# Softmax sums of the first block's heads taken from the four score chunks on TensorE, and later casts and w_out copies on ScalarE

## The chip, the cores and the metric

The kernel runs on one core of one Trainium2 chip. The metric is the device time of one execution in microseconds; a measured time is the median of several runs. Each core has TensorE (PE in the profile: matmuls and, as PEld, the loading of their weights), VectorE (DVE), ScalarE (ACT), GpSimd (POOL), and SyncE (SP), whose queue issues most transfers. Every engine works through its own instructions in the order in which they are written for it.

## The reference

Three layers follow one another: attention with capped scores, a feed-forward layer with a squared ReLU, and a mixture of experts with soft slots.

```python
def _attn_ref(q, k, v, cap):                 # q, k, v: (4, 12, 448, 64)
    scores = scale * np.matmul(q, k.transpose(0, 1, 3, 2))
    scores = cap * np.tanh(scores / cap)
    scores = scores - np.max(scores, axis=-1, keepdims=True)
    attn = np.exp(scores)
    attn = attn / (np.sum(attn, axis=-1, keepdims=True) + 1e-09)
    return np.matmul(attn, v).astype(np.float32)

def _moe_ref(x, w_in, w_out, s, b):          # x: (1792, 768), w_in: (768, 2048), w_out: (2048, 768)
    h = x @ w_in
    r = np.maximum(h, 0.0)
    g = s * (r * r) + b
    return (g @ w_out).astype(np.float32)

def _moe2_ref(x, phi, w1, w2):               # 8 experts, 4 slots each
    logits = x @ phi
    ...
    slot_input = d.T @ x                     # d: softmax of the logits over the tokens
    ...
        h = np.maximum(slot_input[e] @ w1[e], 0.0)
        slot_out[e] = h @ w2[e]
    ...
    return (c @ slot_out).astype(np.float32) # c: softmax of the logits over the slots
```

w_in and w_out come as 64-bit floats, and the kernel turns them into 32-bit ones itself.

## The kernel before

**Pairs of heads.** Attention goes by pairs of heads: 24 pairs, numbered 0 to 23, six for each of the four batch entries. One pair's scores are made in four chunks of 112 keys (`scores`, L111, tile `sc`), each chunk for both heads at once: six matmuls, because the operands q and k are each split into a high part rounded to the matmul format and a low rest (`split`, L72 the cast and L73 the subtraction; tiles `qh`, `ql`, `kh`, `kl`). ScalarE applies tanh to each chunk (L114), and after every second chunk exp to the two together (`expo`, L147); the result is the tile `e`, half 0 for the chunks 0 and 1, half 1 for 2 and 3.

**Softmax sums.** VectorE adds the four chunks into the tile `es` (`add`, L153 for half 0, L156 twice for half 1). `weighted` then makes, per pair, two matmuls of a block of ones with `es` (L165, tile `Sm`), whose 113th row holds the small constant of the reference, and eight matmuls of v with the chunks (L168, tile `U`, one accumulator). One head writes the upper and one the lower 64 partitions of both accumulators. A 32-bit matmul shows as two instructions in the profile. VectorE takes the reciprocal of `Sm` (L172), multiplies (L174), and splits the result into the tile `x` of the feed-forward layer (L72, L73).

**Stages.** In the opening stretch only attention runs: the six pairs of batch entry 0 and the first half of the scores of pair 6, with some of the weight conversion between (`convert`: a piece of w_in or w_out is loaded into `raw`, scaled by ScalarE at L228, and put together by VectorE at L233, L255 and L259; two `raw` buffers). Then come four blocks, one per batch entry: each has 16 chunks of the hidden layer (`hidden`, L380, tile `hp`; the weights are split at L364 by ScalarE and L365 by VectorE), mixed with the next batch entry's attention and with what follows the hidden layer. w_out's pieces are also turned on TensorE (`wturn`, L329, tile `tw`), copied back by VectorE (L331) and stored. In block 3 and behind it the expert weights are loaded and used.

**What sets the order.** A scheduler of the language orders each engine's instructions ahead of time, from the program's order and its own estimates. The chip then follows these lists. The tiles `sc` have two PSUM buffers in the opening stretch and one after it; `U`, `Sm` and the general bank `T` have one each.

Of the kernel before, what the change touches and what calls it, by code (L numbers as in the profile page):

```python
# [18 lines left out]
B, H, S, D = 4, 12, 448, 64  # L19
NP = H // 2  # L20
CP = 112
# [14 lines left out]
CAP_FAST = 40.0  # L36
GP = 3
STEPS = 8
LEAD = 4
U = 256  # L40
CU = 768
# [11 lines left out]
class Body:  # L53
# [14 lines left out]
    def bank(self, name):  # L68
        return self.pst[0].tile([P, 512], F32, tag="T", bufs=self.pst[1], name=name)

    def split(self, hi, lo, src):
        self.nc.vector.tensor_copy(hi, src)  # L72
        self.nc.vector.tensor_sub(lo, src, hi.bitcast(F32))  # L73

    def turns(self, tag, i, kept, more, last, shape, dt):
# [18 lines left out]
    def prep_pair(self, p):  # L94
        if p >= B * NP:
            return
        q2, k2, v = self.qk[p]
        t = [self.ap.tile([P, S], F32R, tag=n, bufs=2, name=n) for n in ("qh", "ql", "kh", "kl")]
        self.split(t[0], t[1], q2)
        self.split(t[2], t[3], k2)  # L100
        self.qk[p] = (*t, v)

    def scores(self, p, c):
# [54 lines left out]
    def weighted(self, p):  # L158

        nc, c = self.nc, self.c  # L160
        U = self.psa.tile([P, 512], F32, tag="U", bufs=1, name="U")
        Sm = self.psa.tile([P, 512], F32, tag="S", bufs=1, name="Sm")
        v = self.qk[p][-1]
        for i in range(2):
            nc.tensor.matmul(Sm[64 * i:64 * i + 64, :S], c["ones"][:CP + 1, :64], self.es[:CP + 1, i, :], start=True, stop=True)  # L165
        for k in range(NCH):
            for i in range(2):
                nc.tensor.matmul(U[64 * i:64 * i + 64, :S], v[:, i, k * D:(k + 1) * D], self.chunk(2 * p + i, k),  # L168
                                 start=(k == 0), stop=(k == NCH - 1))
        del self.qk[p], self.e[p]  # L170
        rec = self.ap.tile([P, S], F32, tag="rec", bufs=1, name="rec")
        nc.vector.reciprocal(rec, Sm[:, :S])  # L172
        u = self.ap.tile([P, S], F32, tag="u", bufs=1, name="u")
        nc.vector.tensor_mul(u, U[:, :S], rec)  # L174
        xt = self.xtile(p // NP)
        self.split(xt[:, 0, p % NP, :], xt[:, 1, p % NP, :], u)

    def xtile(self, bi):
        if bi not in self.x:
# [4 lines left out]
    def attention(self):  # L184

        for p in range(2):
            self.load_pair(p)
        self.prep_pair(0)
        self.es = self.ap.tile([P, 2, S], F32, name="es")
        self.nc.vector.memset(self.es, EPS)  # L190
        if not self.general:
            self.nc.vector.tensor_scalar(self.es, self.es, self.c["eps"], None, op0=ALU.mult)
        last = B * NP
        for p in range(last + 1):
            for k in range(STEPS):
                if p < last and k % 2 == 0:
                    if k == 0:
                        self.load_pair(p + 1)
                    self.scores(p, k // 2)
                    self.expo(p, k // 2)  # L200
                elif k == 3 and p:
                    self.weighted(p - 1)
                elif k in (5, 7) and p < last:
                    if k == 7 or not self.general:
                        for h in range(2) if self.general else (k // 7,):
                            self.add(p, h)
                    if k == 5:
                        self.prep_pair(p + 1)
                yield
# [68 lines left out]
    def conv_units(self):  # L278


        nc, io, c = self.nc, self.io, self.c
# [16 lines left out]
        def proj(fh, half):  # L298
            if half == 0:
                return  # L300
            o = cur.pop(("o", fh)).rearrange("p (a b) -> p a b", b=U)
            self.later = [lambda: down(fh, o)]
            if self.f64:
                self.later += [lambda th=th: wturn(fh, th, o) for th in range(3)]
            self.later.insert(2, lambda: fold(fh))
# [19 lines left out]
        def wturn(fh, th, o):  # L325
            tw = self.bank("tw")
            for j in range(2):
                for k in range(2):
                    nc.tensor.transpose(tw[:, (2 * j + k) * P:(2 * j + k + 1) * P], o[:, 2 * th + k, j * P:(j + 1) * P], c["idn"])  # L329
            n = o[:, 2 * th:2 * th + 2, :].rearrange("p a b -> p (a b)")  # L330
            nc.vector.tensor_copy(n, tw)  # L331
            nc.sync.dma_start(self.osc[th][:, 2 * U * fh:2 * U * (fh + 1)], n)
            self.wide = th < 2

# [184 lines left out]
    def run(self):  # L519
        nc, tc, c = self.nc, self.tc, self.c  # L520
        with ExitStack() as top:
            pool = lambda st, name, side, **k: st.enter_context(tc.tile_pool(name=name, bufs=1, side=side, **k))
            self.gp = pool(top, "gp", "left")
            with ExitStack() as mid:
# [8 lines left out]
                with ExitStack() as att:  # L533
# [5 lines left out]
                    with tc.tile_pool(name="ps2", bufs=1, space=PSUM, side="right") as self.ps2:  # L539
                        for k in range(NP * STEPS + 4):  # L540
                            next(atn)
# [26 lines left out]
    def block(self, bi, atn):  # L568
# [3 lines left out]
        last = bi == B - 1  # L572
        done, total = 0, 0 if last else NP * STEPS
        for grp in range(4):
# [6 lines left out]
            for k in range(12):  # L581
                next(h)
                next(post, None)
                if bi < 2:
                    next(self.conv, None)
                while done < min(total, (12 * grp + k + 1) * total / (48 - LEAD)):
                    next(atn)
# [232 lines left out]
```

## Time and profile before

| | |
|---|---|
| time, median of 3 runs | 693.3 us (691.75 to 693.62) |
| the profiled execution: its time, its span | 692.1 us, 690.2 us |
| TensorE busy | 629.7 us, 91% of the span |
| VectorE busy | 415.9 us, 60% |
| ScalarE busy | 383.5 us, 56% |
| granted TensorE clock, mean | 0.97 |

The span runs from the first to the last instruction of the trace; 1.9 us of the execution lie around it. A busy share is a mean over stages with different limits, and a TensorE that counts as busy may still be waiting inside a pipelined matmul, so the stages have to be read one by one. A granted clock of 1.00 is the level of 2.4 GHz, 0.50 that of 1.2 GHz.

### The profile page before, as it was taken

How to read it: one execution, taken by the hardware profiler on the slowest of the kernel's cores; microseconds unless marked ns; L12 is line 12 of the kernel's file. 1: busy time of each engine (PE TensorE's matmuls, PEld its weight loads, DVE VectorE, ACT ScalarE, POOL GpSimd, SP SyncE). 2: the span in 40 equal slices, each digit the busy share in tenths (PEclk: the TensorE clock that was granted, in tenths of full speed). 3: DMA queues.
4: the chain of work that ended last, by engine and by line, in shares of the span. 5: the costliest groups of instructions: out<-in, count | busy, mean ns of one | idle time of the engine just before them, and what ended most of it. 6: DMA issues, size and time to landing. Idle time of an engine off the chain costs nothing.

```text
span 690.2 us, 10609 instructions
## 1 busy us (share of the span) xinstructions
PE 629.7 (91%) x4222; PEld 396.6 (57%) x4222; DVE 415.9 (60%) x651; ACT 383.5 (56%) x610; POOL 4.6 (1%) x12
## 2 busy tenths in 40 slices
PE   4869999999999999999999999999999986987663
PEld 2324555555555756656667566667868862426553
DVE  5999998989989688664664766654242214102121
ACT  4958676675856756746677467775535561010011
POOL 2000000000000000000000000000000000000000
PEclk9879999999999999999999999999999997899997
DMA  7523367575867462322233123101678839999999
GB/s 238 191 88 123 125 230 255 180 257 199 267 213 269 148 223 82 104 68 59 83 108 95 39 86 106 49 24 47 216 288 291 295 133 366 414 420 418 417 413 299
DMA packets 45640, 136.75 MB, mean 198 GB/s; under 512 B 4352, under 2 KB 23184, under 8 KB 38672
## 3 DMA queue, kind: packets, MB, share of 16 engines
q1 hardware_dynamic: 43136, 120.60, 49.4%
q10 hardware_dynamic: 2016, 14.68, 6.0%
q8 instruction: 35, 0.57, 0.3%
q0 software_dynamic: 432, 0.72, 0.3%
q14 instruction: 21, 0.17, 0.1%
HBM read 117.90 MB, written 18.09 MB: 197 GB/s over the span
## 4 chain that ended last, share of the span: by engine, by line
PE 70%; DMA 15%; DVE 8%; ACT 3%; issue 1%; SPq 0%; ACTq 0%
PE hp L380 32%; DMA wt<-in_w_dram 11%; PE U L168 11%; PE sc L111 9%; PE tp L395 4%; PE Sm L165 3%; PE pt L467 2%; DMA wr<-wsc 2%; PE L L409 2%; DVE rec L172 2%; PE tw L329 2%; DVE es L156 1%; PE si_ps L627 1%; DMA raw<-in_w_in_dram 1%; PE pp L311 1%
## 5 line engine op out<-in xcount | busy, mean ns | idle before, releaser
L380 PE MATMUL hp<-x,ws 128*128 128x448 f32 x1152 | 281.7, 382 | 1.1 <-ACT ws L364 0.8
L380 PEld LDWEIGHTS hp<-x,ws 128*128 128x128 f32 x1152 | 203.6, 188 | 62.7 <-issue 43.4
L114 ACT ACTIVATE e<-sc,c_tsc 112x896 f32<-112x896 f32 x96 | 96.1, 1008 | 55.9 <-PE sc L111 55.0
L365 DVE TENSOR_TENSOR ws<-wr,ws 128x384 fp32r<-128x384 f32 x128 | 70.4, 554 | 93.6 <-ACT ws L364 93.3
L168 PE MATMUL U<-e,v 112*64 112x448 f32 x384 | 96.6, 561 | 10.5 <-DVE u L174 6.6
L364 ACT CAST ws<-wr 128x384 fp32r<-128x384 f32 x128 | 65.0, 510 | 64.1 <-PE hp L380 51.6
L147 ACT ACTIVATE e<-e,c_acap 112x1792 f32<-112x1792 f32 x48 | 86.0, 1792 | 1.0
L172 DVE RECIPROCAL rec<-Sm 128x448 f32<-128x448 f32 x24 | 70.9, 2954 | 15.7 <-PE Sm L165 15.5
L168 PEld LDWEIGHTS U<-e,v 112*64 112x64 f32 x384 | 30.2, 140 | 59.3 <-issue 50.0
L156 DVE TENSOR_TENSOR es<-es,e 112x896 f32<-112x896 f32 x48 | 52.2, 1087 | 16.9 <-ACT e L147 16.6
L111 PE MATMUL sc<-qh,kh 64*112 64x448 f32 x192 | 47.8, 464 | 7.8 <-DVE kh L72 6.2
L397 ACT COPY g<-tp 112x256 f32<-112x256 f32 x128 | 41.7, 378 | 18.4 <-PE tp L395 18.2
L385 ACT ACTIVATE r<-hp 128x448 f32<-128x448 f32 x64 | 35.0, 547 | 27.1 <-PE hp L380 26.9
L111 PEld LDWEIGHTS sc<-qh,kh 64*112 64x112 f32 x192 | 18.6, 178 | 42.8 <-issue 22.2
L395 PE MATMUL tp<-c_cst,r 128*112 128x128 f32 x256 | 39.5, 275 | 3.0 <-ACT r L386 2.0
L111 PE MATMUL sc<-qh,kl 64*112 64x448 f32 x192 | 40.0, 391 | 0.4 <-DVE kl L73 0.4
L111 PE MATMUL sc<-ql,kh 64*112 64x448 f32 x192 | 40.0, 386 | 0.0
L386 ACT ACTIVATE r<-r 128x448 f32<-128x448 f32 x64 | 37.3, 583 | 0.3
L395 PEld LDWEIGHTS tp<-c_cst,r 128*112 128x112 f32 x256 | 29.6, 133 | 12.7 <-ACT r L386 3.1
L689 ACT COPY wt<-op 128x512 f32<-128x512 f32 x12 | 7.0, 586 | 53.1 <-PE op L684 53.1
L672 DVE COPY c_tmp<-so_ps 128x256 f32<-128x256 f32 x6 | 2.5, 424 | 40.0 <-PE so_ps L668 40.0
L165 PE MATMUL Sm<-es,c_ones 113*64 113x448 f32 x96 | 25.0, 580 | 0.7 <-DVE es L156 0.7
(136 smaller groups left out, 582.7 us busy)
## 6 DMA issues: line engine op xcount, KB each, us to landing
wt<-in_w_dram SPq DMA_DIRECT2D x40, 1024.0 KB, 19.9
wr<-wsc SPq DMA_DIRECT2D x48, 384.0 KB, 3.3
raw<-in_w_in_dram SPq DMA_DIRECT2D x16, 768.0 KB, 5.1
raw<-in_w_outT_dram SPq DMA_DIRECT2D x16, 768.0 KB, 5.1
wt<-in_w_dram ACTq DMA_DIRECT2D x8, 1024.0 KB, 7.0
wsc<-wr SPq DMA_DIRECT2D x16, 384.0 KB, 2.8
osc<-o SPq DMA_DIRECT2D x24, 256.0 KB, 2.6
wt<-osc ACTq DMA_DIRECT2D x6, 1024.0 KB, 5.7
```

Source lines behind the costliest of these rows:

```text
L111: nc.tensor.matmul(sc[:, i, :S], k[r, c * CP:(c + 1) * CP], q[r, :], start=(j == 0), stop=(j == 2))
L114: nc.scalar.activation(self.e[p][-1][:, :, c % 2, :], sc[:, :, :S], AF.Tanh, scale=self.c["tsc"][:CP])
L147: self.nc.scalar.activation(e, e, AF.Exp, scale=self.c["acap"][:CP])
L156: nc.vector.tensor_add(es, es, e[:, :, k, :])
L165: nc.tensor.matmul(Sm[64 * i:64 * i + 64, :S], c["ones"][:CP + 1, :64], self.es[:CP + 1, i, :], start=True, stop=True)
L168: nc.tensor.matmul(U[64 * i:64 * i + 64, :S], v[:, i, k * D:(k + 1) * D], self.chunk(2 * p + i, k), start=(k == 0), stop=(k == NCH - 1))
L172: nc.vector.reciprocal(rec, Sm[:, :S])
L364: self.nc.scalar.copy(hi, u)
L365: self.nc.vector.tensor_sub(lo, u, hi.bitcast(F32))
L380: nc.tensor.matmul(hp[:, :S], ws[kc // 3][:, w, kc % 3, :], x[:, s, kc, :], start=(k == 0), stop=(k == 3 * KC - 1))
L395: self.nc.tensor.transpose(tp[:CP, q * P:(q + 1) * P], r2[:, q * CP:(q + 1) * CP], self.c["idn"])
L397: self.nc.scalar.copy(self.g[q][:CP, :, fc * P:(fc + 1) * P], tp[:CP, 2 * q * P:2 * (q + 1) * P].rearrange("p (a b) -> p a b", b=P))
```

## The change

There are three edits. For the pairs 0 to 5 (`DIRECT`) VectorE no longer adds the chunks: `weighted` accumulates eight more matmuls of ones with the four chunks into `Sm`, in front of the two with `es`, whose chunk rows are zero there. For the pairs from 6 on (`CASTS`) the cast of each split is made by ScalarE and only the subtraction by VectorE. And the 24 copies of w_out's turned pieces go from VectorE to ScalarE.

```diff
+DIRECT = NP
+CASTS = NP
...
-    def split(self, hi, lo, src):
-        self.nc.vector.tensor_copy(hi, src)
+    def split(self, hi, lo, src, p):
+        (self.nc.vector.tensor_copy if p < CASTS else self.nc.scalar.copy)(hi, src)
         self.nc.vector.tensor_sub(lo, src, hi.bitcast(F32))
...
-        self.split(t[0], t[1], q2)
-        self.split(t[2], t[3], k2)
+        self.split(t[0], t[1], q2, p)
+        self.split(t[2], t[3], k2, p)
...
+        for k in (3, 2, 1, 0) if p < DIRECT else ():
+            for i in range(2):
+                nc.tensor.matmul(Sm[64 * i:64 * i + 64, :S], c["ones"][:CP, :64], self.chunk(2 * p + i, k), start=(k == 3), stop=False)
         for i in range(2):
-            nc.tensor.matmul(Sm[64 * i:64 * i + 64, :S], c["ones"][:CP + 1, :64], self.es[:CP + 1, i, :], start=True, stop=True)
+            nc.tensor.matmul(Sm[64 * i:64 * i + 64, :S], c["ones"][:CP + 1, :64], self.es[:CP + 1, i, :], start=(p >= DIRECT), stop=True)
...
-        self.split(xt[:, 0, p % NP, :], xt[:, 1, p % NP, :], u)
+        self.split(xt[:, 0, p % NP, :], xt[:, 1, p % NP, :], u, p)
...
+        self.nc.vector.memset(self.es[:CP], 0.0)
...
-                    if k == 7 or not self.general:
+                    if p >= DIRECT and (k == 7 or not self.general):
...
-            nc.vector.tensor_copy(n, tw)
+            nc.scalar.copy(n, tw)
```

The scheduler lays out the lists anew, which moves work beyond these lines. The line numbers of the changed kernel are 2 to 6 higher.

The first place is TensorE's list at pair 3, from the last score chunk ahead of its weighted sums (that chunk belongs to pair 4) to the next score chunk. Before:

```order
L111 MATMUL sc<-qh,kh 112x448 x2
L111 MATMUL sc<-ql,kh 112x448 x2
L111 MATMUL sc<-qh,kl 112x448 x2
L168 MATMUL U<-e,v 64x448 x6
L165 MATMUL Sm<-es,c_ones 64x448 x2
L168 MATMUL U<-e,v 64x448
```

And in the changed kernel:

```order
L113 MATMUL sc<-qh,kl 112x448 x2
L173 MATMUL U<-e,v 64x448
L168 MATMUL Sm<-e,c_ones 64x448 x8
L170 MATMUL Sm<-es,c_ones 64x448 x2
L173 MATMUL U<-e,v 64x448 x7
L113 MATMUL sc<-qh,kh 112x448 x2
```

Before, six of the eight `U` matmuls stood ahead of the sums (a seventh between the score chunks); now one stands ahead, and the ten matmuls of the sums, of which the first already reads the last chunk of exp, come before the other seven. The pairs 1 and 2 have the same list; at the pairs 4 and 5 three `U` matmuls stand ahead of the sums and five behind. Pair 0 has four `U` matmuls ahead, ten of the sums, and four behind.

The second place is ScalarE's list around pair 2, from the tanh of its chunks 0 and 1 to the exp of its second half. Before (the two chunks' tanh, exp, tanh of the chunks 2 and 3, exp, then the scaling of a w_in piece, `wr<-raw`):

```order
L114 ACTIVATE e<-sc,c_tsc 112x2x448
L147 ACTIVATE e<-e,c_acap 112x1792
L114 ACTIVATE e<-sc,c_tsc 112x2x448 x2
L147 ACTIVATE e<-e,c_acap 112x1792
L228 ACTIVATE wr<-raw 128x768
```

In the changed kernel:

```order
L116 ACTIVATE e<-sc,c_tsc 112x2x448 x2
L234 ACTIVATE wr<-raw 128x768
L149 ACTIVATE e<-e,c_acap 112x1792
L234 ACTIVATE wr<-raw 128x768
L116 ACTIVATE e<-sc,c_tsc 112x2x448 x2
L149 ACTIVATE e<-e,c_acap 112x1792
```

Two scalings of w_in pieces moved in front of the tanh of pair 2's chunks 2 and 3. The second of them waits for a load whose `raw` buffer VectorE gives back with the OR that ends the conversion of w_out's first two pieces (L265 of the changed kernel); in VectorE's list that OR is the eleventh instruction behind the `u` of pair 0.

The third place is ScalarE's list at the second half of pair 4, where the casts of pair 6 stand (`kh` and `qh`). Before:

```order
L114 ACTIVATE e<-sc,c_tsc 112x2x448 x2
L147 ACTIVATE e<-e,c_acap 112x1792
```

In the changed kernel:

```order
L116 ACTIVATE e<-sc,c_tsc 112x2x448
L74 CAST kh<-k_552 128x448
L116 ACTIVATE e<-sc,c_tsc 112x2x448
L74 CAST qh<-q_551 128x448
L149 ACTIVATE e<-e,c_acap 112x1792
```

One cast stands between the two tanh and one between the second tanh and exp; at pair 5 it is the same with the casts of pair 7.

## Rows read from the trace of the kernel before

**Rows 1.** Busy time in stretches (length, then each engine; then clock, DMA share, GB/s).
```profile
11.30:14.80 3.50, 0.00 (x0) 0.00 (x0) 1.55 (x3) 2.60 (x3) 0.00 (x0) 0.92 1.02 390
14.80:21.40 6.60, 6.58 (x22) 2.84 (x24) 6.60 (x10) 6.44 (x7) 0.00 (x0) 0.53 0.62 203
34.90:38.50 3.60, 0.03 (x2) 0.00 (x0) 3.60 (x3) 3.18 (x3) 0.00 (x0) 0.95 0.59 207
38.50:48.70 10.20, 8.50 (x26) 3.20 (x28) 9.73 (x15) 4.71 (x4) 0.00 (x0) 0.52 0.26 72
38.80:43.80 5.00, 3.60 (x10) 1.48 (x12) 5.00 (x10) 0.94 (x2) 0.00 (x0) 0.50 0.18 46
70.00:80.00 10.00, 9.20 (x52) 4.10 (x54) 10.00 (x12) 6.80 (x7) 0.00 (x0) 1.00 0.30 91
90.00:478.00 388.00, 384.50 (x2118) 238.44 (x2118) 285.30 (x424) 261.13 (x410) 0.54 (x1) 1.00 0.42 139
```

**Rows 2.** Timeline of TensorE and ScalarE at pair 3 (start, duration, instructions merged).
```profile
50.45 0.46 PE L111 MATMUL sc<-qh,kh 64*112 64x448 f32 x2
...
51.14 0.37 PE L111 MATMUL sc<-qh,kh 64*112 64x448 f32 x2
...
51.35 1.91 ACT L114 ACTIVATE e<-sc,c_tsc 112x896 f32<-112x896 f32 x2 [3.63 <-PE sc L111]
...
53.29 1.79 ACT L147 ACTIVATE e<-e,c_acap 112x1792 f32<-112x1792 f32 x1
...
57.56 0.97 PE L165 MATMUL Sm<-es,c_ones 113*64 113x448 f32 x4 [0.71 <-DVE es L156]
...
59.22 0.46 PE L111 MATMUL sc<-qh,kh 64*112 64x448 f32 x2
```

**Rows 3.** Timeline of TensorE, pairs 0 and 1.
```profile
20.50 2.73 PE L168 MATMUL U<-e,v 112*64 112x448 f32 x10
23.16 0.46 PE L111 MATMUL sc<-qh,kh 64*112 64x448 f32 x2
...
29.11 3.23 PE L168 MATMUL U<-e,v 112*64 112x448 f32 x16 [1.24 <-DVE u L174]
32.27 0.46 PE L111 MATMUL sc<-qh,kh 64*112 64x448 f32 x2
```

**Rows 4.** Groups by line: busy us, mean ns; idle before, releaser.
```profile
L364 ACT CAST ws<-wr 128x384 fp32r<-128x384 f32 x128 | 65.0, 510 | 64.1 <-PE hp L380 51.6 <-DMA wr<-wsc 6.0 <-PE U L168 4.1
L156 DVE TENSOR_TENSOR es<-es,e 112x896 f32<-112x896 f32 x48 | 52.2, 1087 | 16.9 <-ACT e L147 16.6
L331 DVE COPY o<-tw 128x512 f32<-128x512 f32 x24 | 16.3, 680 | 6.4 <-PE tw L329 6.1
L72 DVE CAST x<-u 128x448 fp32r<-128x448 f32 x24 | 9.3, 388 | 0.2
L689 ACT COPY wt<-op 128x512 f32<-128x512 f32 x12 | 7.0, 586 | 53.1 <-PE op L684 53.1
L172 DVE RECIPROCAL rec<-Sm 128x448 f32<-128x448 f32 x24 | 70.9, 2954 | 15.7 <-PE Sm L165 15.5 <-PE U L168 0.2
```

**Rows 5.** Timeline: one load of a raw piece, and ScalarE's first use of it.
```profile
35.18 0.33 SPq L223 DMA_DIRECT2D raw<-in_w_in_dram  x1
...
39.32 0.91 ACT L228 ACTIVATE wr<-raw 128x768 f32<-128x768 f32 x1 [1.21 <-DMA raw<-in_w_in_dram]
```

**Rows 6.** Timeline of TensorE: pair 5's third score chunk, and the change to block 0.
```profile
68.23 0.46 PE L111 MATMUL sc<-qh,kh 64*112 64x448 f32 x2
...
78.02 0.66 PE L329 MATMUL tw<-c_cst,o 128*128 128x128 f32 x4
78.43 1.47 PE L380 MATMUL hp<-x,ws 128*128 128x448 f32 x6
79.83 0.46 PE L111 MATMUL sc<-qh,kh 64*112 64x448 f32 x2
...
80.63 1.49 PE L380 MATMUL hp<-x,ws 128*128 128x448 f32 x6
```

## The prediction

> **What bounds the kernel now.** I read the windows first [rows 1]. From 90 to 478 us TensorE is busy for 384.5 of 388.0 us at a clock of 1.00, VectorE for 285.3 and ScalarE for 261.1. There TensorE is the bound, and all that other engines could give back is the 3.5 us in which it stood idle. The opening stretch, up to about 78 us, is different. From 70 to 80 us VectorE is busy for 10.00 of 10.00 us and TensorE for 9.20; from 34.9 to 38.5 us TensorE does next to nothing while VectorE is full, and in the 10.2 us behind that it runs at a clock of 0.52. So the opening stretch is where VectorE limits the kernel, and the change takes work off VectorE there and puts work on TensorE. Whether that pays depends on what TensorE waits for next.
>
> The timeline at pair 3 [rows 2] shows the chain of one pair. The third score chunk starts at 50.45. Tanh of it starts 0.90 us later, the two tanh take 1.91, exp of both starts at 53.29 and takes 1.79: exp is done 4.63 us after the third chunk's start. Only then can the last two chunks be summed or weighted. The sums (L165) start at 57.56, and the row says what they waited for: VectorE's adds, for 0.71 us. The next pair's third chunk starts at 59.22. So a pair took 8.8 us here.
>
> **What the parts cost.** A matmul of the `U` or `Sm` kind, for both heads, takes 0.75 us at full clock: sixteen instructions, four chunks of both heads, start at 29.11 and the next kind at 32.27, 3.16 us [rows 3], which is 4 x 0.75 and some 0.1 for the change of kind. The first edit adds four such pairs of matmuls per pair of heads: 3.0 us, times six 18.0 us on TensorE. It removes three adds of about 1.09 us [rows 4] per pair: 3.3 us, times six 19.6 us on VectorE. Its extra memset, of one operand less than an add over the same elements, costs between nothing and that add's 1.09. It lies at about 9 us, ahead of a stretch in which VectorE is busy for 1.55 of 3.50 us [rows 1]; that pause hides it, and without the pause it would delay the list by its own length. I take nothing.
>
> The casts of 18 pairs, three each, leave VectorE at 0.388 us each: 21 us. On ScalarE no cast of 448 columns is shown. A cast of 384 takes 0.510, which is the lower bound; in proportion it is 0.595, the upper one. I take 0.55, as a part of an instruction's time is fixed: 54 x 0.55 = 30 us. The 24 copies cost 0.680 on VectorE and, by a copy of the same shape, 0.586 on ScalarE [rows 4]: 14 us. So ScalarE gets 44 us more in some 400 us and would be at about 79% where it is at 67%.
>
> The Trainium skill ("ScalarE: Activation LUTs", What ACT_TABLE_LOAD costs) gives an ACTIVATE with immediate operands 186 ns plus 0.833 ns per column, which would be 0.506 us for 384 columns and 0.559 for 448. The trace's 0.510 agrees at 384, so the sum would stay as it is.
>
> **The opening stretch, step by step, with the changed lists.** Up to 20.50 us nothing differs that TensorE would see.
>
> *Pair 0.* At 20.50 TensorE used to run five `U` matmuls, and pair 1's third chunk followed at 23.16 [rows 3]. Now `U`, ten sums and four `U` stand there: fifteen matmuls, up to eight on one half of the array, 8 x 0.75 = 6.0. The clock is low until 21.4 [rows 1], which costs 0.5 more. Pair 1's third chunk starts at 27.0: 3.8 us later than before.
>
> *Pairs 1 and 2.* The changed list has one `U`, then ten sums, then seven `U`. The first sum reads the last chunk, so it waits for exp: 4.65 us after the third chunk. Behind it stand nine matmuls per half, 6.75, and 0.1 for the change of kind. One round is 11.5 us, in which TensorE waits for ScalarE and then ScalarE for TensorE. Before, up to seven `U` matmuls filled the wait; the adds came at its end. Pair 2's third chunk starts at 38.5 (before: 32.27).
>
> *The load in front of tanh.* In pair 2's round two scalings of w_in pieces stand on ScalarE ahead of the tanh. The second needs a load that waits for the eleventh VectorE instruction behind pair 0's `u`. That `u` ends at about 30.1 (sums of pair 0 done at 25.6: 0.5 of low clock and six matmuls of 0.75; the reciprocal 2.95 [rows 4]; then an OR and `u`, some 1.5). Ten instructions of this mix took 5.00 us [rows 1], so eleven take 5.5 to 6.1, and the load goes out at 36.0. A load took 4.1 us from its issue to the scaling's start [rows 5]: 40.1, and 0.9 for the scaling: 41.0. The tanh could have started at 39.4. It waits 1.6 us (0 to 2.5), and everything on TensorE stands behind it, as the next score chunks need the tanh's buffer. Pair 3: 38.5 + 11.5 + 1.6 = 51.6 (before 50.45, since the old list lost its time just ahead of this, in the idle and low-clock stretch).
>
> *Pair 3* has the plain round: pair 4 starts at 63.1 (before 59.22).
>
> *Pairs 4 and 5.* Here the casts of later pairs stand between tanh, tanh and exp: 2 x 0.55, so exp is done at 5.75. Three `U` fill part of the wait. Behind it come five sums and at most three `U` per half: 6.0, and 0.1. Rounds of 11.9: 75.0 and 86.9. Before, these points were 68.23 and 78.02 [rows 6]. The opening stretch ends **8.9 us later**.
>
> **The rest.** Block 0's first `hp` matmuls, the turns and what follows are the same work, and from there TensorE is the bound, so the delay is carried to the end: the later loads and the tail only start later. Two things change it. The new list has 473 runs of one kind of matmul from the first `hp` on where the old one has 488. A change of kind costs 0.1 to 0.3: a score chunk between `hp` runs takes 0.80 (79.83 to 80.63 [rows 6]), where one directly before another took 0.69 (50.45 to 51.14 [rows 2]), and it has two such changes. Fifteen fewer, at 0.2, give 3 us back (1.5 to 4.5). And the 3.5 us of idle may shrink with VectorE's relief or grow with ScalarE's load: -2 to +4, I take nothing. The cover here is the score wait: in this stretch `sc` has one buffer, and if a cast or a copy stands just ahead of a tanh, the next chunk waits 0.55 us for each.
>
> Sum: 692.1 + 8.9 - 3 = 698.0 for an execution like the profiled one. That one lies 1.2 us below the median of 693.3, so I predict **699.2 us** for the median, its own range 694 to 704.
>
> **The rivals.** *VectorE's relief counts in full (faster).* If the sums hid in the waits, TensorE's work alone would set the end of the opening stretch: from 27.0 five pairs at 6.75 and twenty score chunks at about 0.6 and some 1.4 us for changes of kind, 47.2, end at 74.2, 3.8 us before 78.0. With the 3 us of fewer changes: 686.5. For it speaks that VectorE is full at 70 to 80 us; against it that the changed list has hardly anything left to run while exp is made. It decides where the sums start less than 2 us after the fourth chunk. The Trainium skill ("Perfetto Trace Analysis", Optimization Strategy and Optimizing Scalar/DVE Operations) tells to relieve the most contended engine first and to offload a saturated VectorE; by that rule this case would be the likeliest. The trace agrees that VectorE is full, but not that TensorE has time to spare behind it. Chance 0.12.
>
> *The two cancel (no change).* The same lists, but without the wait for the load, with a round of 11.0 instead of 11.5 and 11.9 as the matmuls of both halves slide into each other, and 4.5 us back later: 8.9 - 1.6 - 2.9 - 1.5 = 2.9, and 1 or 2 us of idle gone: 694. Chance 0.16.
>
> *The clock falls in the opening stretch (slower still).* After 11.3 to 14.8 and 34.9 to 38.5, two stretches without matmuls, the clock was 0.5 for 6.6 and 10.2 us [rows 1]. In the new list TensorE has, from about 40 to 45 us, only two chunks and one `U`. If the clock falls there for some 10 us, the matmuls behind take twice as long: 5 us more, 704. The Trainium skill ("TensorE: Matmul & The Clock Gate", HAM oscillation) warns of just such pauses. Against it: the new list has no such stretch wholly without matmuls. Chance 0.15.
>
> *ScalarE becomes the bound of blocks 0 to 2 (slower).* 54 casts and 24 copies; if one in ten of them and more delays a chunk by 0.55 to 0.9, that is 5 us: 703. Its 79% speak for some of it. Chance 0.10.
>
> **Chances.** The forecast has 0.47. A measurement of this kernel tells 0.3%, 2.1 us, from no change. Slower by more holds the forecast and the last two rivals: 0.72; within it 0.16; faster 0.12. The range reaches to 691 at the low end, which takes in the case where the two cancel, and to 706 at the high end, the fallen clock with a longer wait for the load; what is left out is the fast case and some tail.
>
> **What the profile would show.** Right: adds gone from VectorE before 85 us, and VectorE well under full; sums that start right behind exp, with TensorE waiting for ScalarE; third chunks about 11.5 to 12 us apart; the first `hp` near 88; ScalarE waiting for a w_in load at about 40; no longer any 0.5 clock between 22 and 80; TensorE idle for no more than some 5 us from 95 to 485. It would be wrong if the rounds are 10 us or less, or if TensorE's idle time in the blocks grows by more than 4 us.

## The result and the profile after

The changed kernel took **699.7 us**, median of 5 executions (698.56 to 700.75), beside 693.3 for the kernel before (691.75 to 695.03): a ratio of 1.009, 95% interval 1.0071 to 1.0109. It is slower, as forecast. Its profiled execution is the median one: 699.71 us, span 697.8.

The stages, read first again as busy time in stretches (columns as in [rows 1]):

```profile
21.40:40.00 18.60, 17.85 (x100) 7.36 (x96) 15.97 (x20) 12.69 (x13) 0.00 (x0) 1.00 0.63 198
40.00:45.00 5.00, 3.13 (x18) 1.28 (x18) 4.96 (x10) 4.96 (x5) 0.00 (x0) 1.00 0.78 263
70.00:80.00 10.00, 9.51 (x54) 3.81 (x50) 5.76 (x6) 6.46 (x7) 0.00 (x0) 1.00 0.16 46
95.00:485.00 390.00, 388.74 (x2164) 244.97 (x2163) 261.76 (x353) 295.89 (x489) 0.54 (x1) 1.00 0.41 136
```

VectorE is relieved: from 70 to 80 us it works for 5.76 us where it was full. The stretch at half clock from 38.5 to 48.7 us of [rows 1] is gone: the clock is 1.00 in all four rows. And yet each pair of heads takes longer, but for the one that held that half clock (the rounds stand in the table of the experiments). This is pair 3 in the timeline of TensorE and ScalarE, the place of [rows 2]:

```profile
51.53 0.46 PE L113 MATMUL sc<-qh,kh 64*112 64x448 f32 x2
...
52.44 1.91 ACT L116 ACTIVATE e<-sc,c_tsc 112x896 f32<-112x896 f32 x2 [4.27 <-PE sc L113]
...
53.49 0.46 PE L113 MATMUL sc<-qh,kh 64*112 64x448 f32 x2 [0.48 <-ACT e L116]
...
54.37 1.79 ACT L149 ACTIVATE e<-e,c_acap 112x1792 f32<-112x1792 f32 x1
...
55.19 0.96 PE L173 MATMUL U<-e,v 112*64 112x448 f32 x2
...
56.22 3.23 PE L168 MATMUL Sm<-e,c_ones 112*64 112x448 f32 x16
...
59.28 0.92 PE L170 MATMUL Sm<-es,c_ones 113*64 113x448 f32 x4
60.03 3.18 PE L173 MATMUL U<-e,v 112*64 112x448 f32 x14
63.14 0.46 PE L113 MATMUL sc<-qh,kh 64*112 64x448 f32 x2
```

The third chunk starts at 51.53, exp ends at 56.16, the first sum starts at 56.22, 4.69 us behind the chunk. What stands behind it lasts until 63.14: 6.92 us. The round is 11.61 us. One `U` matmul is all that TensorE has to do between the score chunks and the sums; it ends at 56.15, just as exp does, so that TensorE hardly waits for exp here. The one wait that the rows list is 0.48 us for a tanh, at 53.49.

The wait for the load, in the same timeline with the transfer queue (SPq):

```profile
35.66 0.33 SPq L229 DMA_DIRECT2D raw<-in_w_in_dram  x1
```
```profile
40.00 0.94 ACT L234 ACTIVATE wr<-raw 128x768 f32<-128x768 f32 x1 [3.90 <-DVE rec L177]
40.85 1.88 ACT L116 ACTIVATE e<-sc,c_tsc 112x896 f32<-112x896 f32 x2
41.89 0.46 PE L113 MATMUL sc<-qh,kh 64*112 64x448 f32 x2 [1.76 <-ACT e L116]
```

The releaser named, VectorE's `rec`, ended just then, but the scaling doesn't use it. It reads `raw`, whose load went out at 35.66, 4.34 us earlier (4.14 in [rows 5]), and in a second profile of the same kernel the same wait ends with the load by name:

```profile
39.91 0.92 ACT L234 ACTIVATE wr<-raw 128x768 f32<-128x768 f32 x1 [2.73 <-DMA raw<-in_w_in_dram]
```

TensorE's next chunk (41.89) waits 1.76 us for the tanh behind that scaling, where the plain round has 0.48. In the second profile pair 1's round holds a wait for a load as well: the rounds of the pairs 1 and 2 are 12.72 and 12.32 us there, 11.77 and 12.88 in the first.

The work that moved, as groups by line:

```profile
L74 ACT CAST x<-u 128x448 fp32r<-128x448 f32 x18 | 10.2, 566 | 12.6 <-DVE u L179 12.3
L337 ACT COPY o<-tw 128x512 f32<-128x512 f32 x24 | 14.1, 588 | 8.8 <-PE tw L335 8.6
```

Where the 7.6 us between the two spans (690.2 and 697.8) arose, by the starts of `hp` matmuls, the landing of the last load of expert weights in the chain that ended last, and the end:

| stretch | before | after | difference | forecast |
|---|---|---|---|---|
| start to first `hp` | 78.43 | 87.42 | +9.0 | +8.9 |
| blocks 0 to 2 | 408.95 | 403.08 | -5.9 | -3 |
| block 3, first to last `hp` | 79.05 | 79.85 | +0.8 | 0 |
| last `hp` to the last load's landing | 107.33 | 107.83 | +0.5 | 0 |
| behind that landing | 16.44 | 19.61 | +3.2 | 0 |

### The profile page after: what moved, and what is told of

It is laid out like the page before. It is cut to its first block, busy times and chain, and to the rows that moved or that the text cites. A ratio compares the mean times of both kernels' runs of the same rounds, so it can differ in the third digit from the quotient of the medians.

```text
span 697.8 us, 10792 instructions
## 1 busy us (share of the span) xinstructions
PE 645.4 (92%) x4318; PEld 409.9 (59%) x4318; DVE 370.6 (53%) x556; ACT 416.3 (60%) x688; POOL 4.6 (1%) x12
## 4 chain that ended last, share of the span: by engine, by line
PE 70%; DMA 15%; ACT 8%; DVE 3%; issue 1%; SPq 0%; ACTq 0%
PE hp L386 30%; DMA wt<-in_w_dram 11%; PE U L173 10%; PE sc L113 8%; PE tp L401 4%; PE Sm L170 3%; PE pt L473 2%; PE Sm L168 2%; ACT e L149 2%; DMA wr<-wsc 2%; PE L L415 2%; PE tw L335 2%; ACT e L116 2%; DMA raw<-in_w_in_dram 2%; PE pp L317 1%
## 5 line engine op out<-in xcount | busy, mean ns | idle before, releaser
L173 PE MATMUL U<-e,v 112*64 112x448 f32 x384 | 93.1, 549 | 4.1 <-ACT e L149 4.1
L113 PE MATMUL sc<-qh,kh 64*112 64x448 f32 x192 | 45.9, 460 | 10.3 <-DVE kh L74 6.1
L158 DVE TENSOR_TENSOR es<-es,e 112x896 f32<-112x896 f32 x36 | 39.3, 1091 | 24.6 <-ACT e L149 24.3
L674 PE MATMUL so_ps<-wt,xt 128*32 128x128 f32 x384 | 16.5, 305 | 13.7 <-DMA wt<-in_w_dram 13.7
L170 PE MATMUL Sm<-es,c_ones 113*64 113x448 f32 x96 | 28.6, 558 | 0.0
```

Source lines behind the costliest of these rows:

```text
L113: nc.tensor.matmul(sc[:, i, :S], k[r, c * CP:(c + 1) * CP], q[r, :], start=(j == 0), stop=(j == 2))
L158: nc.vector.tensor_add(es, es, e[:, :, k, :])
```

## The experiments

The table has all kernels, the two unchanged ones twice; rounds are from one pair's third score chunk to the next's (pairs 1 to 5; before, the one marked * holds the idle stretch and the half clock), all starts from the timeline. "Idle" is the length of blocks 0 to 2 less TensorE's busy time there, by windows as above; "changes" counts the runs of one kind of matmul in TensorE's list from the first `hp` to block 3.

| kernel | rounds | first `hp` | blocks 0 to 2 | idle | changes | behind last landing | ratio to before (95%) |
|---|---|---|---|---|---|---|---|
| before | 9.11, 18.17*, 8.77, 9.01 | 78.43 | 408.95 | 3.50 | 397 | 16.44 | 1 |
| after | 11.77, 12.88, 11.61, 11.65 | 87.42 | 403.08 | 1.26 | 382 | 19.61 | 1.0090 (1.0071 to 1.0109) |
| sums alone | 11.79, 12.87, 11.61, 11.62 | 87.98 | 403.26 | 1.10 | 390 | 17.23 | 1.0070 (1.0046 to 1.0093) |
| casts and copies alone | 9.11, 17.77*, 8.78, 7.31 | 78.56 | 403.83 | 5.96 | 370 | 18.71 | 0.9969 (0.9946 to 0.9992) |
| sums from chunk 0 on | 11.67, 11.68, 10.58, 11.35 | 84.39 | 403.28 | 1.53 | 382 | 19.15 | 1.0050 (1.0029 to 1.0071) |
| narrow sums | 9.75, 9.40, 6.75, 12.95 | 74.21 | 403.45 | 1.71 | 382 | 18.65 | 0.9909 (0.9879 to 0.9939) |
| `U` ahead | 10.88, 12.87, 10.59, 11.37 | 85.07 | 402.96 | 1.25 | 382 | 19.54 | 1.0102 (1.0069 to 1.0136) |
| three raw buffers | 6.11, 17.40, 11.62, 11.64 | 85.78 | 400.95 | 3.00 | 368 | 19.34 | 1.0037 (1.0019 to 1.0055) |
| half the sums | 10.14, 10.40, 6.13, 14.49 | 77.54 | 404.67 | 2.67 | 382 | 19.18 | 0.9938 (0.9912 to 0.9964) |
| half, `U` ahead | 9.11, 10.14, 11.22, 10.20 | 76.83 | 404.01 | 4.65 | 372 | 18.29 | 0.9931 (0.9906 to 0.9956) |
| the same, three raw buffers | 11.16, 9.07, 11.87, 10.20 | 77.97 | 399.58 | 1.94 | 368 | 19.06 | 0.9901 (0.9870 to 0.9932) |
| half the sums alone | 10.14, 10.26, 6.14, 14.39 | 77.15 | 403.84 | 1.68 | 390 | - | 0.9909 (0.9878 to 0.9939) |
| before again | 9.13, 17.77*, 8.78, 9.01 | 77.58 | 408.79 | 3.19 | 397 | 16.48 | 0.9993 (0.9971 to 1.0015) |
| after again | 12.72, 12.32, 11.62, 11.65 | 87.31 | 403.79 | 2.00 | 382 | 19.07 | 1.0074 (1.0045 to 1.0103) |

Where one round is short and the next long, the list only holds the marking chunk on the other side of the sums; their mean counts. In half the sums alone another piece of work lies behind the last landing, so its tail is left out. Two profiles of one kernel differ by up to 0.85 us in the first `hp` and by up to 0.7 in the blocks and their idle time, so smaller differences between kernels say nothing; the blocks less their idle time repeat within 0.15.

**The two halves of the change.** The first edit alone, and the second and third alone:

```diff
-CASTS = NP
+CASTS = B * NP
...
-            nc.scalar.copy(n, tw)
+            nc.vector.tensor_copy(n, tw)
```


> The first edit alone: TensorE makes the sums of the pairs 0 to 5, all casts and w_out copies stay on VectorE. Theory (the sums stand on TensorE right behind exp, so TensorE and ScalarE take turns, and each round is 4.65 us to the end of exp plus what is queued behind it): rounds of 11.5 to 11.7 us as in the full change, first hp at 86 to 88 us, time 698 to 702. Rival (the casts and copies on ScalarE cost the time): first hp before 82, time 695 or less.

```diff
-DIRECT = NP
+DIRECT = 0
```


> The second and third edit alone: VectorE adds the chunks again for all pairs, casts from pair 6 on and the w_out copies on ScalarE. Theory: the opening stretch is as before, first hp at 77 to 80 us, and the blocks are 1 to 3 us shorter than before: 690 to 693. Rival (casts and copies cost the time): 697 or more.

The sums alone took 698.1 us and make the whole of the long opening; pair 4's round is 11.62 without ScalarE's casts between the tanh and 11.65 with them, and from pair 5's third chunk to the first `hp` it is 12.60 and 12.63, so those casts cost nothing there. Casts and copies alone took 692.2 and leave the rounds as before. The shorter blocks come with either edit alone (with the casts and copies 5.1 us, where 1 to 3 were expected) and are not shorter with both. Casts and copies alone make TensorE stand still for 5.96 us in the blocks, though, and block 3 lasts 82.50 us there (79.05 before): ScalarE waits for its weights, as the waits from 525 to 560 us show (engine, line, releaser; us in all, times, longest; before, in the same window, the same wait has 4.8 us in 3 places):

```profile
ACT ws L370 <- DMA wr<-wsc: 10.1, 4, 4.6
```

**Is it the place of the sums or their amount?** The first kernel writes the sums from chunk 0 to chunk 3, so that the four of the chunks 0 and 1 can start ahead of the second exp:

```diff
-        for k in (3, 2, 1, 0) if p < DIRECT else ():
+        for k in range(NCH) if p < DIRECT else ():
...
-                nc.tensor.matmul(Sm[64 * i:64 * i + 64, :S], c["ones"][:CP, :64], self.chunk(2 * p + i, k), start=(k == 3), stop=False)
+                nc.tensor.matmul(Sm[64 * i:64 * i + 64, :S], c["ones"][:CP, :64], self.chunk(2 * p + i, k), start=(k == 0), stop=False)
```


> The full change, but the eight added matmuls take the chunks in the order 0, 1, 2, 3, so that half of them need only the first exp and can run while the second is made; the same matmuls, the same number. Theory (turn taking): behind exp stand 7 matmuls per half of the array instead of 9, rounds of 10.0 to 11.0 instead of 11.6, first hp 4 to 6 us earlier, at 81 to 83, time 693 to 697. Rival (TensorE's 18 us of added work is the cost, in whatever order): within 1 us of the full change, 699 to 700.5.

It took 697.1 us, and the first `hp` came 3.0 us earlier than in the changed kernel, at 84.39 where 81 to 83 were expected. The place counts, but for less than expected: in pairs 1 and 2 a scaling and the next pair's tanh also stand ahead of exp in ScalarE's new list, and only pair 3, without these, came to 10.58. There TensorE does not wait for exp at all: the first sum starts at 53.74, exp of the second half ends at 54.72, and no idle time is listed from 52.05 to the end of the round. Pair 4's round is longer by 0.77 us, and what differs is one head's sum by itself between two score chunks:

```profile
63.41 0.96 PE L168 MATMUL Sm<-e,c_ones 112*64 112x448 f32 x2
```

The second keeps order and number of the matmuls and makes the eight added sums narrow (so it leaves the sums of batch entry 0 out):

```diff
-                nc.tensor.matmul(Sm[64 * i:64 * i + 64, :S], c["ones"][:CP, :64], self.chunk(2 * p + i, k), start=(k == 3), stop=False)
+                nc.tensor.matmul(Sm[64 * i:64 * i + 64, :CP], c["ones"][:CP, :64], self.chunk(2 * p + i, k)[:, :CP], start=True, stop=True)
...
-            nc.tensor.matmul(Sm[64 * i:64 * i + 64, :S], c["ones"][:CP + 1, :64], self.es[:CP + 1, i, :], start=(p >= DIRECT), stop=True)
+            nc.tensor.matmul(Sm[64 * i:64 * i + 64, :S], c["ones"][:CP + 1, :64], self.es[:CP + 1, i, :], start=True, stop=True)
...
-        self.nc.vector.memset(self.es[:CP], 0.0)
+        self.nc.vector.memset(self.es[:CP], 1.0)
```


> The changed kernel with its order, but the eight added sums of each pair are 112 columns wide instead of 448 and the two with es overwrite them: it leaves the softmax sums of batch entry 0 out. The same number of matmuls stands behind exp, with about 0.2 us instead of 0.75 for each of four per half. Theory (wait for exp plus the duration of what stands behind it): rounds shorter by 4 x 0.55 = 2.2, 9.3 to 9.5 us; first hp at 76 to 79, time 688 to 692. Rival (the rounds are set by VectorE's or ScalarE's turn, and the matmuls' length is hidden): rounds stay above 11, first hp at 85 to 88, time 697 to 701.

It took 686.65 us, less than the 688 to 692 expected, with the first `hp` at 74.21 (76 to 79 expected). Its timeline at pair 2:

```profile
34.73 0.46 PE L113 MATMUL sc<-qh,kh 64*112 64x448 f32 x2
...
39.44 0.99 PE L168 MATMUL Sm<-e,c_ones 112*64 112x112 f32 x16
40.26 0.92 PE L170 MATMUL Sm<-es,c_ones 113*64 113x448 f32 x4
41.01 3.18 PE L173 MATMUL U<-e,v 112*64 112x448 f32 x14
44.12 0.46 PE L113 MATMUL sc<-qh,kh 64*112 64x448 f32 x2
```

From chunk to sums 4.71 us, as after the change; the sixteen instructions then last 0.82 instead of 3.06, and the round is shorter by just that: 9.39. Over five rounds to the first `hp` it is 49.2 instead of 60.5, 2.3 a round. The length of the sums counts in full. That is what turn taking gives, but a TensorE that is its own bound gives it too, so this kernel does not tell the two apart.

The third writes `U` of the chunks 0 and 1 ahead of them:

```diff
+        for k in range(2 if p < DIRECT else 0):
+            for i in range(2):
+                nc.tensor.matmul(U[64 * i:64 * i + 64, :S], v[:, i, k * D:(k + 1) * D], self.chunk(2 * p + i, k), start=(k == 0), stop=False)
         for k in (3, 2, 1, 0) if p < DIRECT else ():
...
-        for k in range(NCH):
+        for k in range(2 if p < DIRECT else 0, NCH):
```


> All of the changed kernel, but the weighted sums of the chunks 0 and 1 (four U matmuls) are written ahead of the ten matmuls of the sums, so they stand in the list between the fourth score chunk and the first sum. Theory (a round is 4.65 us to the end of exp plus what stands behind exp): seven matmuls per half behind exp instead of nine, 4.65 + 5.25 + 0.1 = 10.0 us a round where the changed kernel has 11.65; with the load wait in pair 3's round the first hp comes 6 to 8 us earlier, at 79.5 to 82, and the time is 692 to 695. Rival (TensorE's amount of work sets the rounds, wherever it stands): rounds stay at 11.6, first hp at 87 to 88, time 698 to 701.

The theory missed. Apart from the one with the load wait, the rounds fell to 10.6 to 11.4 and not to 10.0; the median, 698.7 us, is no better than that of the changed kernel (its executions go from 696.7 to 703.6, and the profiled one, with its first `hp` 2.3 us earlier, is the fastest). The rival, rounds of 11.6, missed too. Its timeline at pair 3:

```profile
50.74 0.46 PE L113 MATMUL sc<-qh,kh 64*112 64x448 f32 x2
...
52.71 0.46 PE L113 MATMUL sc<-qh,kh 64*112 64x448 f32 x2 [0.48 <-ACT e L116]
...
53.60 1.79 ACT L149 ACTIVATE e<-e,c_acap 112x1792 f32<-112x1792 f32 x1
...
54.41 1.72 PE L168 MATMUL U<-e,v 112*64 112x448 f32 x8
55.97 3.18 PE L171 MATMUL Sm<-e,c_ones 112*64 112x448 f32 x16
...
59.73 1.67 PE L176 MATMUL U<-e,v 112*64 112x448 f32 x8
61.33 0.45 PE L113 MATMUL sc<-qh,kh 64*112 64x448 f32 x2
```

The sums start 5.23 us behind the chunk, when exp has been done for 0.58 us (it ends at 55.39). From 52.71 on TensorE stands nowhere: two chunks of the next pair, `U`, sums, `U`. So in this order the round is TensorE's own work but for the 0.48 us in front of 52.71, and some 10.6 us is what it costs with all of the sums, as in pair 3 with the sums from chunk 0 on. The changed kernel's round is 1.0 us longer with the same matmuls: there one head's `U` stands alone ahead of the sums (0.96 us). Its exp's end (56.16) and TensorE's own arrival (`U` from 55.19) fall on the same moment; there is hardly a wait for exp to take away.

**The wait for the load.**

```diff
-        self.raws = 2
+        self.raws = 3
```


> The changed kernel with three raw buffers instead of two, so that the load ahead of pair 2's scaling need not wait for VectorE's OR behind pair 0's u. Theory (the load wait is the 1.2 us by which that one round is longer than the others): the round between the third chunks of pairs 2 and 3 is 11.5 to 11.8 us instead of 12.88, the wait for the load is gone, and the first hp comes 1 to 1.5 us earlier, at 86 to 86.7; time 697 to 699.5. Rival (the wait only moves to another load, since VectorE is not earlier): the round stays at 12.5 to 13 or another becomes that long, first hp at 87.3 to 88, time 699 to 701.

From pair 1's third chunk to pair 3's it took 23.50 us instead of 24.65 (25.04 in the changed kernel's second profile): the waits for loads were worth 1.15 to 1.5. The first `hp` came 1.6 us earlier. The time, 695.5 us, fell by more than expected; blocks 0 to 2 took 400.95 us, with fewer changes of kind in the list.

**Half of the sums.** VectorE adds the chunks 0 and 1, as before, and TensorE sums the result and the chunks 2 and 3, so that two of VectorE's three adds go and four of the eight matmuls stay:

```diff
-        for k in (3, 2, 1, 0) if p < DIRECT else ():
+        for k in (3, 2) if p < DIRECT else ():
...
-                    if p >= DIRECT and (k == 7 or not self.general):
+                    if k == 7 or not self.general:
                         for h in range(2) if self.general else (k // 7,):
-                            self.add(p, h)
+                            if h == 0 or p >= DIRECT:
+                                self.add(p, h)
```


> The full change, but VectorE adds the chunks 0 and 1 (one add of 1.06 us, ready long before the second exp) and TensorE takes only the chunks 2 and 3 directly: six matmuls for the sums instead of ten, 9 us less of added work, and no add behind exp. Theory (turn taking): rounds of 9 to 10.2 us, first hp at 75 to 78, time 687 to 692. Rival (only the amount of TensorE's work counts): 9 us less than the full change, 690 to 691.5. Rival (VectorE limits again): rounds as before or longer, time 693 or more.

689.7 us: faster than both kernels. The first `hp`, at 77.54, is as expected, the mean of the four rounds, 10.29, just above. But the rival that counts only the amount of TensorE's work, 9 us less than 87.42, comes to 78.4, so this kernel does not decide between the two. Then the same without the second and third edit:

> The halved first edit alone: VectorE adds the chunks 0 and 1, TensorE sums that and the chunks 2 and 3; casts and w_out copies stay with VectorE. If the opening stretch and the blocks are independent, this keeps the opening of the halved kernel with ScalarE's casts (first hp at 77.5, within 0.7) and loses what the casts gave by themselves in blocks 0 to 2 (they took 403.8 us instead of 409 with the casts and copies alone, but 403.3 also with the sums alone): 690 to 692. Rival (the blocks' gain comes from any new list, not from VectorE's relief): blocks 403 to 405 us and 689 to 690.

The opening is the same, and the time is 687.6, lower than expected: nothing is lost when casts and copies go back to VectorE. The rival was right about the blocks, 403.84 us, though not about the time.

With `U` of the chunks 0 and 1 ahead, as above:

> VectorE adds the chunks 0 and 1, TensorE sums that and the chunks 2 and 3 (six matmuls of sums instead of ten), and the four U matmuls of the chunks 0 and 1 stand ahead of them. Theory: five matmuls per half behind exp, 4.65 + 3.75 + 0.1 = 8.5 us a round (up to 9.3 where VectorE's u of the pair before, which frees U, comes late); first hp at 72 to 76, time 684 to 689. Rival (VectorE is the bound of the opening stretch again once a third of its adds is back): rounds not under 10.1, the mean of the kernel with half of the adds and its own order; first hp at 77 to 79, time 689 to 691.

688.5 us, as expected, but the first `hp` at 76.83 is outside what the theory gave. Only pair 1's round, 9.11, is the plain one. In the rounds of pairs 2 and 3 a scaling ahead of a tanh waits for its load:

```profile
35.70 0.89 ACT L238 ACTIVATE wr<-raw 128x768 f32<-128x768 f32 x1 [1.20 <-DMA raw<-in_w_in_dram]
...
47.52 0.93 ACT L238 ACTIVATE wr<-raw 128x768 f32<-128x768 f32 x1 [0.93 <-DMA raw<-in_w_in_dram]
```

A third raw buffer was to take that away:

> The kernel with half of the adds and U of the chunks 0 and 1 ahead of the sums, with three raw buffers instead of two. In the one with two buffers ScalarE waited for a w_in load 1.2 and 0.9 us just ahead of a tanh, in the rounds of pair 2 (10.14 us) and pair 3 (11.22), where pair 1's round took 9.11. Theory (load waits lengthen these two rounds): both shrink to 9.1 to 9.8, the first hp comes 2 to 3 us earlier, at 73.5 to 75, and the time is 685.5 to 688. Rival (the waits only move, since VectorE frees raw no earlier): first hp at 76.5 to 77.5 and 688 to 690.

Pair 2's round fell to 9.07, as expected, but the first `hp` came no earlier (77.97 after 76.83). Pair 1's round rose to 11.16, since the load wait went there. Pair 3's rose to 11.87: `U` waits 1.06 us for VectorE, and then the granted clock is 0.50 from 49.5 to 52.5 us, so that its eight instructions last 3.26 us where the same eight last 1.72 at pair 1:

```profile
29.07 0.93 ACT L238 ACTIVATE wr<-raw 128x768 f32<-128x768 f32 x1 [1.62 <-DMA raw<-in_w_in_dram]
...
31.73 1.72 PE L171 MATMUL Sm<-e,c_ones 112*64 112x448 f32 x8 [1.71 <-ACT e L149]
...
49.54 3.26 PE L168 MATMUL U<-e,v 112*64 112x448 f32 x8 [1.06 <-DVE u L182]
```

Its median, 687.0 us, gives the lowest ratio, 0.990. But the profiled execution is the slowest of its six, 690.6, so the profile does not show where that time was won; in it the blocks are the shortest of all (399.58), while the opening, for which the kernel was made, is no shorter. The intervals of the four halved kernels overlap; all lie below before.

**The end.** Both kernels once more, unchanged:

> The kernel before, unchanged, as one more profile: for the tail. In its first profile the work behind the last load of expert weights took 16.4 us at a mean clock of 0.79, in the changed kernel 19.6 at 0.54, in the others 17.2 to 19.5. Theory (that difference is which clock the last matmuls happen to get, not the change): this profile shows 17 to 19.5 us, with the last hp and the last landing where they were within 0.5 us, and a time of 693 to 696. Rival (the change brings the low clock about): 16.2 to 16.8 us again. The ratio to the kernel before is that of a kernel to itself: 1.000.

> The changed kernel once more, beside the kernel before on the same chip, for its tail and for the interval: time 698.5 to 700.5, ratio 1.007 to 1.011; work behind the last landing 17 to 19.6 us. If the tail of the first profile was its own property, 19.3 to 19.8 us again.

The kernel before took 692.2 us, 0.9993 of itself (0.9971 to 1.0015), the changed one 698.4, 1.0074 (1.0045 to 1.0103). My theory missed for the tail: before showed 16.48 us behind the last landing, as at first, and the changed kernel 19.07. The rows of that stretch for the changed kernel at first, for before again, and for the halved kernel with `U` ahead:

```profile
678.19:697.80 19.61, 10.01 (x92) 9.15 (x92) 3.25 (x7) 2.34 (x4) 0.00 (x0) 0.53 0.75 239
```
```profile
673.52:690.00 16.48, 5.90 (x92) 5.40 (x92) 3.20 (x7) 2.34 (x4) 0.00 (x0) 0.76 0.85 275
```
```profile
669.61:687.90 18.29, 5.89 (x92) 5.39 (x92) 3.19 (x7) 2.34 (x4) 0.00 (x0) 0.76 0.77 250
```

The same 92 matmuls took 10.01 us at the low clock and 5.90 without. But the third row has before's matmul time and still ends 1.8 us later, so the clock is not all of it. The last work in the chain that ended last, a copy of the output, divides the stretch. Here it is for before, the changed kernel, the changed kernel again, and the halved one with `U` ahead:

```profile
679.87 1.09 DVE wt L687 x2
```
```profile
689.10 0.42 DVE wt L693
```
```profile
685.62 1.09 DVE wt L693 x2
```
```profile
675.72 1.09 DVE wt L697 x2
```

| profile | landing to the end of that copy | from there to the end (the last stores) |
|---|---|---|
| before, and before again | 7.2, 7.2 | 9.2, 9.3 |
| after, and after again | 11.3, 8.7 | 8.3, 10.4 |
| half, `U` ahead | 7.2 | 11.1 |

In the changed kernel's first profile the slower matmuls are more than the whole difference; in the second they make 1.5 of 2.6 us and the last stores the other 1.1; in the halved kernel it is the stores alone. Neither piece goes with the change: over the thirteen profiles that can be compared the first is 7.2 us in five, three of them of changed lists, and 8.7 to 11.5 in the others, and the second lies between 7.6 and 11.5.

## Why the prediction was right, step by step

**The opening: right in size and nearly in place.** Pair 1's third chunk came at 26.88 (27.0 forecast), pair 2's at 38.65 (38.5), pair 3's at 51.53 (51.6), pair 4's at 63.14 (63.1), pair 5's at 74.79 (75.0), the first `hp` at 87.42 (86.9). The round's terms, 4.65 to the end of exp and 6.85 behind, measured 4.69 and 6.92. The load went out at 35.66 (36.0), and the tanh behind its scaling started at 40.85 (41.0), 1.3 us late (1.6); the kernel with three raw buffers shows 1.15 to 1.5 for such waits. The rival with a fallen clock did not come true: from 40 to 45 us, where it had the pause, TensorE works for 3.13 of 5.00 us at a clock of 1.00. Two steps there were wrong, and they go opposite ways. The casts between tanh and exp do not lengthen the rounds of the pairs 4 and 5: 11.65, not 11.9, and 11.62 without these casts. And from pair 5's third chunk to the first `hp` it was 12.63, not 11.9, since twelve `pp` matmuls, which its sum did not have, take 0.98 us there:

```profile
86.44 1.06 PE L317 MATMUL pp<-o,c_misc 128*32 128x256 f32 x12
```

**The mechanism: the wait for exp was hardly there.** The prediction said that TensorE waits for ScalarE and then ScalarE for TensorE, and made the round of exp's end plus what stands behind it. The sum is right, but the wait is not what makes it. TensorE reaches the first sum by itself just when exp ends, and it is busy for 17.85 of 18.60 us. Its waits from 21.4 to 95 us are all for the tanh's buffers, in 5 places; the longest is the 1.76 us of the round with the load, where a plain round has 0.48:

```profile
PE sc L113 <- ACT e L116: 3.9, 5, 1.8
```

With `U` ahead, and at pair 3 with the sums from chunk 0 on, exp is out of the way and the round is still 10.6 us, all but 0.5 of it TensorE's own work; the 1.0 us more in the changed kernel is the head that stands alone. Pair 4 says the same: with the casts in front of it exp ends at 68.57, 5.43 us behind the third chunk and not 4.63, two more `U` stand ahead of the sums, and the round stays at 11.65. That the wait for exp and TensorE's own work came to the same 4.69 us was luck for the forecast. No kernel took exp's time away by itself, so how little would be won by it is read from these rows. So the opening went from VectorE's bound to one that is in the main TensorE's own, with 3.9 us of waits for ScalarE in it.

The rival in which relief counts in full put 47.2 us from pair 1's third chunk to the end of the opening; it took 60.5. It left out the 3.9 us of waits, the 0.98 of `pp`, a tenth matmul time of 0.75 in each round for the head that stands alone, and it took a score chunk at 0.6 us where four of them, less the wait, last 3.18 with their changes of kind (51.53 to 55.19). The Trainium skill ("Perfetto Trace Analysis", Identifying the Most-Contended Engine), which the prediction set beside this rival, says to optimize the engine with the highest occupancy first; for a saturated VectorE the same page (Optimizing Scalar/DVE Operations) names ScalarE and GpSimd as engines to offload to, not TensorE. The trace shows that engine relieved (5.76 of 10 us), and every round but the one with the half clock longer, because the work went to an engine with 9.20 of 10 us already taken.

**Blocks 0 to 2: the term was mis-sized.** Forecast -3 with bounds of 1.5 and 4.5 for fewer changes and nothing for idle time; measured -5.9. Idle time fell by 2.2 (3.50 to 1.26), just past the bounds of -2 to +4 that I kept. That leaves 3.6 for 15 fewer changes, 0.24 each where I took 0.2. The 0.2 did not follow from the row that I gave for it: 0.80 against 0.69 is 0.11 for two changes, which would have made the term 0.8. The table supports that fewer changes go with less time, but not in even steps: block time less idle is 405.5 at 397 changes, 402.2 in both kernels with 390, 401.7 to 402.0 in the five with 382, 399.4 at 372, 397.9 at 370, 397.6 and 397.9 at 368. Seven changes fewer than before come with 3.3 us, the next eight with some 0.3. No kernel varied the changes alone, so it is an agreement and not a proof. A rival lies in the trace: the runs of `U` that leave one head's matmul alone are 18 before, 8 after, and 4 in the kernels with 368 changes, and of all kinds `U` lost most. Counted from one instruction's start to the next one's, without idle time, its 288 instructions took 65.9 us before and 63.4 after, the 864 of `hp` 200.6 and 199.2, and `sc` and `Sm` together 76.2 and 76.3. ScalarE's casts measured 0.566 us (0.55 taken) and its copies 0.588 (0.586). But this work was no relief: sums alone and the whole change have the same blocks (403.26 and 403.08), and half of the sums needs no casts on ScalarE. ScalarE at 76% (79 forecast) was no bound either; the rival that makes it one shows itself most in the casts and copies alone, where score chunks wait for a tanh in 3 places, 3.0 us of the 5.96 us of idle time; the changed kernel has no such wait in its blocks.

**From block 3 on: carried unchanged was wrong.** The prediction put the delay through to the end as it was. Measured was 4.5 us more: 0.8 in block 3, 0.5 until the last load landed and 3.2 behind that. Behind that landing the clock of the last matmuls makes up more than all of it in the first profile and 1.5 us in the second, the last stores the rest. Before showed the short tail twice, but other changed lists have its matmul time too; why the clock is lower and the stores longer in some profiles stays open. This error and that of the blocks nearly cancel, which is why the sum, 698.0 for the profiled execution against 699.7, looks better than its terms.

## What to carry to other kernels

When work leaves a full engine, look first at how full the receiving engine is in the same stretch and at what else its list must do there: work that is given to a nearly full engine counts for the most part, wherever it stands. Here another place in the list gave back 2.3 to 3.0 us of the 9.0, and halving the sums 9.9. Splitting the transfer is worth trying, since the half that hides can stay where it is: half of these sums on TensorE beat both all of them and none. And check a forecast by its terms, because a right total can hold two errors of opposite sign.

## What the runs showed that I had not expected

- One head's `U` matmul by itself takes as long as one for each head side by side. At pair 4 of the changed kernel the two instructions of one matmul last 0.97 us and, a little later, the four of two matmuls 0.97 us as well. A list that leaves one head's matmul alone pays for both:

```profile
65.92 0.97 PE L173 MATMUL U<-e,v 112*64 112x448 f32 x2
...
67.61 0.97 PE L173 MATMUL U<-e,v 112*64 112x448 f32 x4
```
- A third raw buffer, meant for one wait of 1.15 us, changed TensorE's list as far as the blocks (368 changes instead of 382), where TensorE's busy time fell from 401.8 to 397.9 us and its idle time rose from 1.3 to 3.0: with a scheduler, a small edit is also a draw of a new order.
- After the last load of expert weights, the same 92 matmuls took 5.9 us in five of the thirteen profiles that can be compared, both of the kernel before among them, and 7.4 to 10.2 in the other eight.
